# Ordering transfers one behind the other, casting four batches ahead, and widening a quarter-array layout to two more batches

## The chip, the cores and the metric

The kernel runs on one core of one Trainium2 chip. The metric is device time in microseconds (us). A run's median and range cover all of its executions. Engines are named as in the profile: PE is the TensorE (PEld its weight loads), DVE the VectorE, ACT the ScalarE, POOL the GpSimd, SP the SyncE, which here only issues transfers.

## The reference

Eight batches, eight heads, 576 positions, 64 features. Each head has two attentions, whose outputs are added: one on q, k and v averaged over groups of four positions, repeated back to 576, and one local, over neighbours closer than four positions. The result, 4608 tokens of 512 features, goes through a two-layer feed-forward block.

```python
def _attn_ref(q, k, v):                       # each (8, 8, 576, 64) fp32
    q_d = q.reshape(B, H, 144, 4, D).mean(axis=3)        # also k_d, v_d
    out_up = np.repeat(sm_attn(q_d, k_d, v_d), 4, axis=2)
    mask = np.abs(pos[:, None] - pos[None, :]) < 4
    ...                                       # softmax of the masked scores, times v
    return out_up + out_local

def _moe_ref(x, w_in, w_out):                 # x (4608, 512), w_in (512, 2048), w_out (2048, 512)
    h = x @ w_in
    g = 0.5 * h * (1.0 + erf(h * inv_sqrt2))
    return g @ w_out
```

## The kernel before

The tokens go through the two layers in nine chunks of 512 rows. In each chunk `m1` is the first layer with its gelu, `m2` the second. The attention of the next batch `b = c + 1` is woven into the second layer: it calls `fill(n)`, which puts n second-layer matmuls between its own short ones, so that the PE has something to do while exponentials and masks are made elsewhere. During `m1` the VectorE prepares the batch (`prep`, or `prep_q` for batches from BQ on): sums of four, and copies of values and keys.

A batch's data come in three steps. The **cast** copies keys and queries from fp32 to fp16 in device memory, on GpSimd's transfer queue. The **transposes** (`qk_turn`) bring them into the on-chip memory with features on partitions, from SP's queue. The **value loads** (`v_load`) are transfers on GpSimd's queue, among them `v_grp` and `v_lo` (values grouped by four) and `v_win` (windows of 64 positions). In the traces each engine goes through its instructions in the order of the program. On GpSimd a one-element copy onto `hold` waits for its operand, and so holds back everything behind it.

```python
def qk_cast(b, names=("kn", "qn")):
    for nm in names:
        t = dpool.tile([S, H, D], F16, tag=f"{nm}{0 if b == 2 else 1 - b % 2}", bufs=1, name=nm[0] + "16")
        nc.gpsimd.dma_start(out=t, in_=(k if nm == "kn" else q)[b].rearrange("h s d -> s h d"))
        v16[nm, b] = t
        ...

def qk_turn(b):
    for nm in ("kn", "qn"):
        nc.sync.dma_start_transpose(out=xT_of(b, nm), in_=v16[nm, b].rearrange("s h d -> s (h d)"))

# one attention on the full array
def attn(b, fill):
    fill(6)
    scores(b, 0)
    s_lo(b)
    fill(6)
    mask(0)
    for p in range(NP):                      # four groups of two heads
        if p + 1 < NP:
            scores(b, p + 1)
            mask(p + 1)
            ...
            fill(2)
        else:
            fill(4)
        av(b, p)                             # values and sums
        norm_out(b, p)
        ...

# ... the main loop
for c in range(NCH):
    b = c + 1
    f1 = filler(m1(c)) if c else f1_0
    ...
    if b == 1:
        qk_turn(2)
        v_load(2)
    elif b < B:
        (prep_q if b >= BQ else prep)(b)
    if 1 < b < B - 1:
        nc.gpsimd.tensor_copy(out=hold, in_=KL[0:1, 0:1] if b < BQ else qd[0:1, 0, 0:1])
        if b < BQ:
            qk_cast(b + 1)
        v_load(b + 1)
        if b == BQ - 1:
            qk_cast(7)
        qk_turn(b + 1)
    f1()
    f2 = filler(m2(c))
    if b < B:
        to_exp()
        (attn_q if b >= BQ else attn)(b, f2)
    f2()
```

For batches 6 and 7 (BQ = 6) the attention runs on quarters: matmuls of 64x64 placed on the four quarters of the 128x128 array, several at once (in the trace of the kernel before four of them start within 0.03 us, at 212.68 us, and take 0.20 us each). That is less time for the PE (an undisturbed stretch, as defined below, takes 32.00 us in place of 32.70) and far more instructions: 437 matmuls per chunk in place of 245.

## Time and profile before

| what | before |
|---|---|
| time, median of 3 runs (range) | 325.49 us (324.43 to 326.04) |
| span of the profiled execution, mean granted clock | 322.9 us, 0.995 |
| PE busy | 312.4 us, 97% |
| stretches of batches 2 to 7 | 33.40, 32.70, 32.70, 32.70, 37.40, 32.00 us |

A stretch goes from the start of one chunk's first layer to that of the next; stretch b carries the attention of batch b. The prediction below shows these lines and reads them. One more view matters for what came after: the timeline of GpSimd in the kernel before, around the preparations of batches 5 and 6 (columns: start, duration, engine, line, operation, output<-input, count, and in brackets the idle time before it with what ended it).

```profile
170.45 0.20 POOL L894 COPY hold<-KL 1x1 f16<-1x1 f16 x1 [11.45 <-DVE KL L347]
170.71 2.21 POOL L167 DMA_DIRECT2D k<-in_k_dram  x1
172.40 2.74 POOL L167 DMA_DIRECT2D q<-in_q_dram  x1
174.10 1.93 POOL L154 DMA_DIRECT2D v_grp<-in_v_dram  x1
...
203.49 0.18 POOL L894 COPY hold<-qd 1x1 f16<-1x1 f16 x1 [6.77 <-DVE qd L386]
203.97 0.91 POOL L154 DMA_DIRECT2D v_grp<-in_v_dram  x1 [0.30 <-issue]
```

Here a batch's grouped values stand behind two cast transfers at most (or none), and are issued a whole stretch before they are summed. The view of that tile has them landing 10.5 to 15.6 us after issue, over seven batches. So in the kernel before no load of grouped values was late: nothing on the PE or the VectorE waited for `v_grp`.

### The profile page before, as it was taken

To read this page: it belongs to the slowest core of one execution; us is meant where nothing else is said; L and a number is where in the kernel's file an instruction comes from. 1 tells how busy PE (TensorE), PEld (TensorE's weight loads), DVE (VectorE), ACT (ScalarE), POOL (GpSimd) and SP (SyncE) were. 2 spreads that over 40 slices of the span, in tenths; PEclk is the share of its full clock that TensorE was granted. 3 is DMA by queue.
4 is the path that set the end of the run, shared out by engine and by line. 5 is a ranking of instruction groups with operands and counts; after the bars stand their busy time and mean duration, and the time that the engine had idled before them with its cause. 6 is when DMAs were issued, how large, how long until landed. Compare 5 with 4: busy or idle time off the path is not lost.

```text
span 322.9 us, 6805 instructions
## 1 busy us (share of the span) xinstructions
PE 312.4 (97%) x2803; PEld 162.0 (50%) x2803; DVE 176.6 (55%) x395; ACT 220.2 (68%) x381; POOL 114.2 (35%) x145
## 2 busy tenths in 40 slices
PE   8899999999999999999999999995999999999995
PEld 3565655544654565446545554452444544444444
DVE  7575777539875757675795479935492640000001
ACT  6676977777886788678867886764576677415610
POOL 8968478332912564065308353630000000000000
PEclk9999999999999999999999999999899999999999
DMA  6999999999999599979999999999200120020011
GB/s 86 147 184 177 202 196 159 163 145 181 124 164 159 145 161 141 185 119 168 147 228 62 173 144 208 167 153 154 98 9 0 37 100 0 0 99 32 0 67 65
DMA packets 155454, 39.96 MB, mean 124 GB/s; under 512 B 137376, under 2 KB 150944, under 8 KB 155424
## 3 DMA queue, kind: packets, MB, share of 16 engines
q0 software_dynamic: 122064, 23.02, 90.0%
q1 hardware_dynamic: 33360, 16.52, 27.9%
q8 instruction: 22, 0.36, 0.5%
q14 instruction: 8, 0.07, 0.1%
HBM read 46.01 MB, written 16.52 MB: 194 GB/s over the span
## 4 chain that ended last, share of the span: by engine, by line
PE 77%; DMA 15%; POOL 3%; issue 2%; DVE 2%; POOLq 0%; DVEq 0%
PE m_ps L283 36%; PE m_ps L252 26%; DMA w_in_sb<-in_moe_w_in_dram 6%; PE m_first L244 4%; DMA q_nat<-q 4%; DMA v_grp<-in_v_dram 3%; DMA w_out_sb<-in_moe_w_out_dram 3%; PE nm L561 2%; PE sc L551 1%; PE sc L533 1%; POOL old L214 1%; PE m_ps L274 1%; PE sc L449 1%; DVE qd L308 1%; PE nm L558 1%
## 5 line engine op out<-in xcount | busy, mean ns | idle before, releaser
L283 PE MATMUL m_ps<-w_out_sb,gT 128*128 128x512 f16 x544 | 128.4, 383 | 0.4 <-DMA w_out_sb<-in_moe_w_out_dram 0.4
L252 PE MATMUL m_ps<-xT,w_in_sb 128*128 128x512 f16 x504 | 111.9, 379 | 0.0
L255 ACT ACTIVATE gT<-m_ps 128x512 f16<-128x512 f32 x126 | 75.2, 597 | 30.7 <-PE m_ps L252 30.5
L283 PEld LDWEIGHTS <-gT 128*128 128x128 f16 x544 | 50.3, 98 | 55.3 <-issue 2.9
L252 PEld LDWEIGHTS <-w_in_sb 128*128 128x128 f16 x504 | 48.6, 98 | 58.0 <-issue 1.4
L144 POOL DMA_DIRECT2D v_win<-in_v_dram x40 | 33.2, 972 | 30.7 <-DMA q<-in_q_dram 14.6
L278 DVE COPY out_sb<-m_ps 128x256 f32<-128x256 f32 x2 | 0.8, 424 | 54.4 <-PE m_ps L274 54.4
L287 ACT COPY out_sb<-m_ps 128x512 f32<-128x512 f32 x21 | 12.3, 584 | 26.0 <-PE m_ps L283 25.8
L576 DVE TENSOR_TENSOR xl<-nm,lr 128x576 f16<-128x576 f32 x20 | 15.2, 758 | 17.5 <-ACT lr L572 17.5
L591 DVE TENSOR_TENSOR xT<-xl,up 128x576 f16<-128x576 f16 (+8 forms) x41 | 22.1, 565 | 0.8
L707 POOL DMA_DIRECT2D v_win<-in_v_dram x20 | 14.6, 896 | 14.6 <-DMA v_grp<-in_v_dram 4.3
L545 DVE TENSOR_TENSOR e<-e,band 128x576 f16<-128x576 f16 x20 | 9.1, 453 | 14.6 <-ACT e L540 14.6
L167 POOL DMA_DIRECT2D q<-in_q_dram x6 | 15.9, 2652 | 0.4 <-DMA w_out_sb<-in_moe_w_out_dram 0.4
L244 PE MATMUL m_first<-xT,w_in_sb 128*128 128x512 f16 x64 | 15.1, 379 | 0.0
L894 POOL COPY hold<-KL 1x1 f16<-1x1 f16 x4 | 0.8, 204 | 40.0 <-DVE KL L347 40.0
L571 ACT ACTIVATE lr<-lr 128x576 f32<-128x576 f32 x20 | 13.7, 683 | 0.6
L247 ACT ACTIVATE gT<-m_first 128x1024 f16<-128x1024 f32 x8 | 8.2, 1024 | 8.6 <-PE m_first L244 8.6
L539 ACT ACTIVATE ed<-sc 128x288 f16<-128x288 f32 x20 | 8.1, 407 | 8.3 <-PE sc L533 8.3
L167 POOL DMA_DIRECT2D k<-in_k_dram x6 | 13.3, 2209 | 0.8 <-DMA v_win<-in_v_dram 0.5
L488 DVE TENSOR_TENSOR xl<-nm,lr 128x576 f16<-128x576 f32 x8 | 6.1, 758 | 13.6 <-ACT lr L484 13.6
L570 ACT ACTIVATE lr<-sc 128x576 f32<-128x576 f32 x20 | 13.1, 657 | 0.0
L540 ACT ACTIVATE e<-sc 128x576 f16<-128x576 f32 x20 | 12.9, 644 | 0.0
(233 smaller groups left out, 475.5 us busy)
## 6 DMA issues: line engine op xcount, KB each, us to landing
out_dram<-out_sb SPq DMA_DIRECT2D x35, 256.0 KB, 5.9
v_grp<-in_v_dram POOLq DMA_DIRECT2D x7, 512.0 KB, 12.4
k<-in_k_dram POOLq DMA_DIRECT2D x6, 576.0 KB, 8.5
q<-in_q_dram POOLq DMA_DIRECT2D x6, 576.0 KB, 11.1
v_win<-in_v_dram POOLq DMA_DIRECT2D x40, 72.0 KB, 9.9
w_in_sb<-in_moe_w_in_dram POOLq DMA_DIRECT2D x4, 512.0 KB, 9.1
w_out_sb<-in_moe_w_out_dram POOLq DMA_DIRECT2D x4, 512.0 KB, 9.0
v_win<-in_v_dram POOLq DMA_DIRECT2D x20, 64.0 KB, 11.6
```

The lines of the kernel that those rows point to most:

```text
L144: nc.gpsimd.dma_start(out=vw[64 * hh:64 * hh + 64, 0:9, p, 64 * hh:64 * hh + 64], in_=bass.AP(x.tensor, x.offset, [[D, 64], [57 * D, 9], [ ...
L167: nc.gpsimd.dma_start(out=t, in_=(k if nm == "kn" else q)[b].rearrange("h s d -> s h d"))
L244: nc.tensor.matmul(out=half[j], lhsT=w_in_sb[:, fc, 128 * j:128 * j + 128], rhs=xT[:, fc, x0:x0 + 512], start=(fc == 0), stop=(fc == 3))
L252: nc.tensor.matmul(out=ps, lhsT=w_in_sb[:, fc, 128 * j:128 * j + 128], rhs=xT[:, fc, x0:x0 + 512], start=(fc == 0), stop=(fc == 3))
L255: nc.scalar.activation(out=g[:, j, :], in_=ps, func=ACTF.Gelu)
L283: nc.tensor.matmul(out=ps, lhsT=g[:, j, 128 * t:128 * t + 128], rhs=w_out_sb[:, j, :], start=(j == 0), stop=(j == NJ - 1))
L540: nc.scalar.activation(out=e.rearrange("p (g c) -> p g c", g=2), in_=sc2[:, :, 0:SH], func=ACTF.Exp, scale=0.125)
L570: nc.scalar.activation(out=lr2, in_=sc2[:, :, 0:SH], func=ACTF.Ln)
L571: nc.scalar.activation(out=lr2, in_=lr2, func=ACTF.Exp, scale=-1.0)
L576: nc.vector.tensor_tensor(out=xl.rearrange("p (g c) -> p g c", g=2), in0=nm2[:, :, 0:SH], in1=lr2, op=ALU.mult)
L591: nc.vector.tensor_tensor(out=xT[:, p, y:y + z - a].rearrange("p (g r) -> p g r", r=4), in0=xl[:, a:z].rearrange("p (g r) -> p g r", r=4), ...
L707: nc.gpsimd.dma_start(out=quarter(b)["vw"][HS[g], i, :, :], in_=v[b, :, w:w + 64, :].rearrange("h s d -> s h d"))
```

## The change

The intent is to take traffic out of the late stretches, where something delayed the PE. The transposes go ahead of the value loads, and each kind of transfer behind the one before it; the casts of 4 to 7 move ahead, into the stretches of batches 2 and 3; batches 4 and 5 also run on quarters. Lesser parts: copies on the VectorE become maxima of an operand with itself, the constants of quarters are made a batch earlier, and the first second layer takes its matmuls in another order. The core of the diff (left out: a tile `bandq` of its own for the mask of quarters, `k_lo` moved up in `prep`, one more filler size):

```diff
-    BQ = 6
+    BQ = 4
@@ qk_cast
-            t = dpool.tile([S, H, D], F16, tag=f"{nm}{0 if b == 2 else 1 - b % 2}", bufs=1, name=nm[0] + "16")
+            t = dpool.tile([S, H, D], F16, tag=f"{nm}{b}", bufs=1, name=nm[0] + "16")
@@
+    def held(x):
+        nc.gpsimd.tensor_copy(out=hold, in_=x)
@@ qk_turn
-        for nm in ("kn", "qn"):
+        for nm in ("kn", "qn") if b == 2 else ("qn", "kn"):
@@ m2 of chunk 0
-            for t in range(2):
-                for j in range(NJ // 2):
+            for t, j0, j1 in ((0, 0, 8), (1, 0, 8), (0, 8, 12), (1, 8, 11)):
+                for j in range(j0, j1):
@@
+    def same(out, x):
+        nc.vector.tensor_tensor(out=out, in0=x, in1=x, op=ALU.max)
+
+    def quarter_consts():
+        ...                                  # moved here from prep_q
@@ attn, on the full array
-        fill(6)
+        fill(8 if b == 2 else 6)
@@ main loop
+        if 1 < b < B:
+            (prep_q if b >= BQ else prep)(b)
+        if b == BQ - 1:
+            quarter_consts()
         if b == 1:
             qk_turn(2)
+            held(xT_of(2, "qn")[0:1, 0, 0:1])
             v_load(2)
-        elif b < B:
-            (prep_q if b >= BQ else prep)(b)
-        if 1 < b < B - 1:
-            nc.gpsimd.tensor_copy(out=hold, in_=KL[0:1, 0:1] if b < BQ else qd[0:1, 0, 0:1])
+        elif b < B - 1:
+            if b == 2:
+                held(KL[0:1, 0:1])
+                qk_cast(3)
+            qk_turn(b + 1)
             if b < BQ:
-                qk_cast(b + 1)
+                held(xT_of(b + 1, "kn")[0:1, 0, 0:1])
             v_load(b + 1)
-            if b == BQ - 1:
-                qk_cast(7)
-            qk_turn(b + 1)
+            for n in {2: (4,), 3: (5, 6, 7)}.get(b, ()):
+                qk_cast(n)
```

## The prediction

> **What bounds the kernel now.** I read the page first, then busy time by stretch, then the order of the TensorE in time. The page says that the TensorE is the bound:
>
> ```profile
> PE 312.4 (97%) x2803; PEld 162.0 (50%) x2803; DVE 176.6 (55%) x395; ACT 220.2 (68%) x381; POOL 114.2 (35%) x145
> PE   8899999999999999999999999995999999999995
> PEclk9999999999999999999999999999899999999999
> DMA  6999999999999599979999999999200120020011
> ```
>
> No other engine passes 68%, so only three things can shorten the span: less TensorE work, a TensorE gap closed, or a slow clock avoided. There is one notch, in slice 28 (index 27, about 218 to 226 us), where the clock digit also dips. The DMA row is full until about 234 us and almost empty after it: transfers are crowded early, and the last third has room.
>
> I then cut the span where the first layer of each 512-row chunk starts (its first pair of banks, m_first). Each stretch is one chunk's two layers with the next batch's attention woven into the second layer. Columns: stretch, length, busy us (instructions) of PE, PEld, DVE, ACT, POOL, then clock, DMA share, GB/s.
>
> ```profile
> 63.10:96.50 33.40, 33.04 (x245) 17.22 (x244) 22.70 (x45) 25.82 (x47) 14.87 (x17) 1.00 1.71 154
> 96.50:129.20 32.70, 32.70 (x245) 17.21 (x244) 21.97 (x41) 25.61 (x47) 15.42 (x18) 1.00 1.56 152
> 161.90:194.60 32.70, 32.70 (x245) 17.23 (x244) 22.09 (x44) 25.61 (x47) 15.25 (x17) 1.00 1.52 150
> 194.60:232.00 37.40, 33.85 (x437) 16.16 (x436) 23.49 (x59) 23.29 (x38) 10.62 (x14) 0.95 1.57 161
> 232.00:264.00 32.00, 32.00 (x437) 15.67 (x436) 20.19 (x45) 23.17 (x39) 0.00 (x0) 1.00 0.10 35
> ```
>
> These carry batches 2, 3, 5, 6 and 7 (batch 4's is 32.70 too). Batches 6 and 7 already use quarters. A full-array stretch costs 32.70, an undisturbed quarter stretch 32.00. Batch 6's took 37.40, so it lost 5.4 us; batch 2's lost 0.7. The order in time shows where batch 6 lost it:
>
> ```profile
> 220.14 0.24 PE L421 MATMUL sc<-qd,kdt 64*64 64x72 f16 x6
> ...
> 223.93 0.22 PE L421 MATMUL sc<-qd,kdt 64*64 64x72 f16 x2 [3.54 <-issue]
> ```
>
> Six of eight score matmuls of one group ran, then nothing for 3.54 us, with no data, engine or buffer named: "issue". A data wait would not split a group whose operands are the same tiles. In program order the stopped instruction is number 4003 of 5608 in the TensorE's queue. The page's instruction queue moved 22 packets:
>
> ```profile
> q8 instruction: 22, 0.36, 0.5%
> ```
>
> 0.36 MB over 22 is 16 KB, that is 256 instructions of 64 bytes. I located all 22 in time and counted the TensorE instructions run by then: 21 come 49 to 173 instructions after numbers 163 + 256k, and one, k = 14, comes 331 after, at about 221 us. The next number of that series is 4003. So the TensorE ran into a block of instructions not yet there: the fetch, due at about 216.4 when the block before it was entered, was over at 223.9, some 7.5 us. The TensorE had crossed a block in under 4 us because quarters need many short instructions. Afterwards it ran half-clocked for a while: twelve second-layer matmuls took 4.38 us in the chain of waits, against 2.70 elsewhere. 3.54 + 1.68 = 5.2 of the 5.4.
>
> Why was the fetch late? Transfers were crowded. In batch 6's stretch the transposes and value windows for batch 7 ran together, after a hold that released only when prep 6 was done at 203.5. Output stores of 256 KB measure it: median time to landing in batch 6's stretch, then in batch 7's:
>
> ```profile
> out_dram<-out_sb SPq DMA_DIRECT2D x6, 256.0 KB, 7.0
> out_dram<-out_sb SPq DMA_DIRECT2D x4, 256.0 KB, 2.2
> ```
>
> [...] an idle of 3.54 us, then 0.79 mean clock from 224 to 232 us. [...]
>
> **The change part by part.**
> 1. *Batches 4 and 5 on quarters.* Two stretches go from 32.70 to 32.00: **-1.4 us**. The TensorE queue grows from 5608 to 6376 instructions, so 3 more block fetches.
> 2. *Casts ahead.* The cast of 4 moves into batch 2's stretch, those of 5, 6, 7 into batch 3's. From batch 4 on nothing holds the transposes and value loads, which start as soon as their buffers are free, at the stretch's start. For batch 6's stretch this leaves one pair of transposes (before: 12.5 to 14 us from issue to landing each) and about 7 us of value loads, begun at its start rather than 9 to 11 us into it. They should be over before attention 6, 14 us in. Attention 6 contains the same block alignment as before (a crossing at the 29th of 96 value and sum instructions, the next at the 13th of 16 score instructions, 3.9 us later), so only a fast fetch saves it. In batch 7's empty stretch four fetches cost nothing. **-5.4 us**.
> 3. *Transposes before value loads (batches 2 to 4).* Before, q of batch 2 landed at 75.8 because it shared engines with value loads; its sum ended at 78.5, and the first score waited 0.28; more went at the mask behind it. Batch 2's keys' sums now also go ahead, and attention starts two fillers later: **-0.5** of the 0.7.
> 4. *Reordered start of the first second layer.* The 0.43 us wait for the last quarter of w_out lay in the chain. Now 23 matmuls, not 20, precede its first use, at 0.216 each 0.65 us more: **-0.4**.
> 5. *Copies turned into maxima.* A 64x512 copy took 0.29; the two-operand form takes 0.68 for that many columns; four of them add 1.6 us of VectorE per quarter batch, the small ones 0.2. Prep 7 ended at 243.4, and value products come after 250. Off the path: **0**. The constants (about 2.4 us) move to batch 3's stretch, ahead of its first mask.
>
> Sum: -7.7 us, giving 317.8.
>
> **The rivals.**
> *The serial chain becomes the bound.* In batches 2 and 3 one transfer now waits for another: transpose pair, value loads (11 or 12 issues at about 0.75, so 9 us), cast (k and q: about 11 us alone). Batch 3's last transpose is now the keys', and the VectorE needs 8 us from there to the queries' sum (1.9 copies, 2.6, 0.6, 0.4, 2.6). Attention 3 wants it at about 110.3, so keys by 102. The cast of 3 starts near 79 to 81 and lands near 91. If an uncrowded pair of transposes takes 8 to 9 us, keys come at 100 and nothing is lost; if it still takes the 12 us of issue alone that it took before (6 + 6.4 to 8), they come at 105, and attention 3 stalls 3 us, the constants before the mask add perhaps 2, and batches 4 and 5 inherit some. That would leave 321 to 323. For it: every pair on record took at least 12 us of issue. Against: all of those were crowded; first packets moved 4.4 us after issue, as stores took 7 instead of 2.
> *The late fetch returns elsewhere.* Casts 5 to 7 (about 22 us of transfers) spill into batch 4's stretch while its attention runs in short instructions. Its crossings are about 6 us apart, against a crowded fetch of 4 to 7.5: 0 to 1.5 us. In attention 5 one pair is 4.1 us apart, when transfers should be done; if not, up to 3.5 plus the clock.
> *The 3.54 us was a data wait.* Then casts cannot cure it and about 323 remains. The arithmetic of 256 speaks against it.
>
> **Range and chances.** I charge 0.8 us for the first two rivals on average: 317.8 + 0.8 = 318.6. Everything clean gives 317; a stall of 3 to 4 us in batches 3 to 5 gives 322. Two per cent is 319.0, hardly above my number, so the verdict hangs on whether these stalls stay below 1.2 us: 0.56 faster, 0.41 same, 0.03 slower.
>
> **What would show it.** Right: no TensorE gap over 1 us after 50 us; stretches of 4, 5, 6 and 7 at 32.0 each, of 2 and 3 below 33; 25 instruction packets; clock 1.00 throughout. Wrong: a first-score or mask wait in batch 3's stretch behind a transpose (serial chain); an "issue" gap in attention 4 or 5 at numbers 163 + 256k (late fetch); batch 6's gap still there (cause misread).

## More of the kernel before

From the first layer, `m1`, the loop that two experiments change:

```python
    for j in range(2, NJ):
        ps = mm()
        for fc in range(4):
            nc.tensor.matmul(out=ps, lhsT=w_in_sb[:, fc, 128 * j:128 * j + 128],
                             rhs=xT[:, fc, x0:x0 + 512], start=(fc == 0), stop=(fc == 3))
            ...                              # gelu after fc == 3
```

## The result and the profile after

| | before | after |
|---|---|---|
| time, median of 4 runs (range; one more run of the kernel before than in the table above) | 325.76 us (324.43 to 328.01) | 338.74 us (337.82 to 341.73) |
| ratio to before, 95% interval | | 1.0407 (1.0319 to 1.0495): slower |
| span of the profiled execution, clock | 322.9 us, 0.995 | 337.5 us, 0.972 |

A ratio is the mean time of one kernel's fast runs over that of the other's in the same rounds, so it is not quite the ratio of the medians in the table. Executions over 1.5% slower than the fastest of the same kernel are left out of the means. The outputs are correct. The change costs 4%; the prediction had it gaining 2%.

The page of the kernel after, with the lines that answer to those which the prediction quotes (busy time by engine, then the span in 40 slices):

```profile
PE 311.6 (92%) x3187; PEld 159.5 (47%) x3187; DVE 175.5 (52%) x400; ACT 215.4 (64%) x365; POOL 113.7 (34%) x144
...
PE   7799999999999999999993069999999999999995
...
PEclk9999999999999999999999559999999999999998
DMA  6999999999999999999999999990100110011011
```

The PE has 0.8 us less to do than before and takes 14.6 us longer: there is one hole, 180.9 to 197.4 us into the span, and a halved clock in it and right after it (0.50 granted from 185.6 to 202.7 us). (The instruction queue moved 25 packets, as predicted.) Batches 2 and 3 took 33.04 and 33.34 us; the busy time by stretch for batches 4 to 6 (start:end, length, busy us and instructions of PE, PEld, DVE, ACT and POOL, then clock, DMA share and GB/s):

```profile
129.83:161.91 32.08, 32.08 (x438) 15.72 (x436) 20.39 (x44) 23.04 (x39) 24.37 (x22) 1.00 1.79 137
161.91:214.02 52.11, 34.99 (x437) 16.85 (x437) 20.97 (x47) 23.32 (x39) 17.92 (x27) 0.84 1.54 158
214.02:246.01 31.99, 31.99 (x437) 15.68 (x437) 20.77 (x44) 23.14 (x39) 4.16 (x7) 1.00 0.66 90
```

Nearly everything that went wrong is in batch 5's stretch. Against before: start of batch 2's stretch (62.93 by the first matmul of its first layer, now 63.45; the prediction cut at 63.10) +0.5, batches 2 to 7 -0.36, +0.64, -0.62, **+19.41**, **-5.41**, -0.02, the rest +0.4; the sum is the 14.6 us of the two spans. Batch 5's 52.11 consists of 32.0 for an undisturbed quarter stretch, 17.1 us in which the PE stood still (52.11 less 34.99 busy) and 3.0 us more busy time at a low clock (34.99 against 31.99, at a granted 0.84 against 1.00).

What did it stand still for? The order of the PE in time, and the VectorE's timeline:

```profile
177.60 0.45 PE L415 MATMUL sl<-qd,ex 128*128 128x144 f16 x4 [0.59 <-DVE ex L375]
...
197.39 0.46 PE L456 MATMUL sc<-e,ON 64*64 64x288 f16 x4 [16.52 <-DVE e L445]
```

```profile
171.84 2.55 DVE L392 TENSOR_REDUCE kdt<-k_nat 128x576 f16<-128x2304 f16 x1 [9.13 <-DMA k_nat<-k]
...
176.77 0.86 DVE L375 TENSOR_TENSOR ex<-kdt 64x32 f16<-64x32 f16 x8
191.19 0.69 DVE L371 TENSOR_TENSOR v_two<-v_grp 128x512 f32<-128x512 f16 x1 [13.56 <-DMA v_grp<-in_v_dram]
...
196.88 0.46 DVE L445 TENSOR_TENSOR e<-e,bandq 128x576 f16<-128x576 f16 x1
```

The PE waits for the masked exponentials `e`. The multiplication that makes them takes 0.46 us and needs no values at all, but it stands on the VectorE behind the sums of batch 5's values, and those wait 13.56 us for `v_grp` to land; the sums and copies behind it fill 191.19 to 196.88. So the VectorE passed a late operand on to work that does not read it. (The keys of batch 5 were late too: the VectorE waited 9.13 us for them, until 171.84. That alone cost the PE the 0.59 us for `ex`.) The chain of waits names the transfer:

```profile
158.58 32.59 DMA v_grp<-in_v_dram
```

From issue to landing 32.59 us, where the median of this tile is 7.0:

```profile
DMA to landing us min/median/max: 6.0/7.0/32.6
```

GpSimd's timeline tells why it was issued so late, and what was ahead of it. The buffers for batch 5's values were free at 129.8 us, when batch 3's attention ended.

```profile
140.14 2.26 POOL L168 DMA_DIRECT2D k<-in_k_dram  x1
...
152.54 2.19 POOL L168 DMA_DIRECT2D k<-in_k_dram  x1 [1.44 <-issue]
156.90 2.20 POOL L168 DMA_DIRECT2D q<-in_q_dram  x1 [2.17 <-issue]
158.58 1.40 POOL L155 DMA_DIRECT2D v_grp<-in_v_dram  x1
...
176.89 0.68 POOL L714 DMA_DIRECT2D v_win<-in_v_dram  x1 [10.69 <-DMA k<-in_k_dram]
188.05 0.68 POOL L714 DMA_DIRECT2D v_win<-in_v_dram  x1 [10.48 <-DMA q<-in_q_dram]
```

Six cast transfers are issued between 140 and 159 us; the grouped values of batch 5 come seventh. Issuing is not landing: at 176.89 and 188.05 GpSimd itself still waits for casts to end. Meanwhile SP issues the transposes of batches 5 and 6, whose packets move beside the casts' (the page counts both queues as shares of the same 16 engines): those of 5 are being issued from 152.3 to 165.5, those of 6 from 167.7 to 182.8. In the packet records GpSimd's queue moves about 1055 packets per us from 152 to 158 us, while SP's moves 82, and about 474 from 158 to 165.5, beside 314 of SP's.

So the traffic that was taken out of batch 6's stretch, which did become as short as predicted, was piled up ahead of batch 5's loads.

### The profile page after: what moved, and what is told of

It reads as the page before. It is cut to its first block, busy times and chain, and to the rows that moved or that the text cites.

```text
span 337.5 us, 7581 instructions
## 1 busy us (share of the span) xinstructions
PE 311.6 (92%) x3187; PEld 159.5 (47%) x3187; DVE 175.5 (52%) x400; ACT 215.4 (64%) x365; POOL 113.7 (34%) x144
## 3 DMA queue, kind: packets, MB, share of 16 engines
q1 hardware_dynamic: 33360, 16.52, 22.7%
HBM read 46.01 MB, written 16.52 MB: 185 GB/s over the span
## 4 chain that ended last, share of the span: by engine, by line
PE 62%; DMA 23%; DVE 8%; POOL 4%; issue 1%; ACT 1%; DVEq 0%; POOLq 0%
PE m_ps L287 29%; PE m_ps L256 22%; DMA v_grp<-in_v_dram 10%; DMA w_in_sb<-in_moe_w_in_dram 6%; DMA w_out_sb<-in_moe_w_out_dram 4%; PE m_first L248 3%; DMA v_win<-in_v_dram 2%; PE sc L456 2%; DMA k_nat<-k 1%; POOL old L218 1%; PE nm L456 1%; PE m_ps L278 1%; PE sc L434 1%; PE nm L568 1%; DVE kdt L308 1%
## 5 line engine op out<-in xcount | busy, mean ns | idle before, releaser
L287 PE MATMUL m_ps<-w_out_sb,gT 128*128 128x512 f16 x537 | 126.1, 384 | 0.0
L714 POOL DMA_DIRECT2D v_win<-in_v_dram x40 | 27.7, 735 | 35.4 <-DMA k<-in_k_dram 10.7
L490 ACT ACTIVATE lr<-sc 128x720 f32<-128x720 f32 x16 | 12.3, 770 | 36.9 <-PE sc L456 35.4
L456 PE MATMUL sc<-e,ON 64*64 64x288 f16 x64 | 5.2, 313 | 16.5 <-DVE e L445 16.5
L145 POOL DMA_DIRECT2D v_win<-in_v_dram x24 | 18.2, 840 | 5.8 <-DMA w_out_sb<-in_moe_w_out_dram 2.3
L168 POOL DMA_DIRECT2D q<-in_q_dram x6 | 15.2, 2533 | 4.2 <-issue 4.2
L168 POOL DMA_DIRECT2D k<-in_k_dram x6 | 14.5, 2410 | 1.7 <-issue 1.7
L445 DVE TENSOR_TENSOR e<-e,bandq 128x576 f16<-128x576 f16 x16 | 7.2, 451 | 15.0 <-ACT e L444 15.0
L392 DVE TENSOR_REDUCE kdt<-k_nat 128x576 f16<-128x2304 f16 x4 | 10.2, 2546 | 9.1 <-DMA k_nat<-k 9.1
L491 ACT ACTIVATE lr<-lr 128x720 f32<-128x720 f32 x16 | 12.8, 803 | 0.5
L371 DVE TENSOR_TENSOR v_two<-v_grp 128x512 f32<-128x512 f16 x8 | 5.5, 688 | 14.5 <-DMA v_grp<-in_v_dram 14.4
```

Source lines behind the costliest of these rows:

```text
L145: nc.gpsimd.dma_start(out=vw[64 * hh:64 * hh + 64, 0:9, p, 64 * hh:64 * hh + 64], in_=bass.AP(x.tensor, x.offset, [[D, 64], [57 * D, 9], [ ...
L287: nc.tensor.matmul(out=ps, lhsT=g[:, j, 128 * t:128 * t + 128], rhs=w_out_sb[:, j, :], start=(j == 0), stop=(j == NJ - 1))
L456: nc.tensor.matmul(out=out(g, hh), lhsT=lhsT(g, hh), rhs=rhs(g, hh), start=start, stop=stop)
L490: nc.scalar.activation(out=lr2, in_=sc2[:, :, 0:SH + DH], func=ACTF.Ln)
L491: nc.scalar.activation(out=lr, in_=lr, func=ACTF.Exp, scale=-1.0)
L714: nc.gpsimd.dma_start(out=quarter(b)["vw"][HS[g], i, :, :], in_=v[b, :, w:w + 64, :].rearrange("h s d -> s h d"))
```

## The experiments

The theory after the result, T: the loss comes from the order in GpSimd's stream, casts 5 to 7 ahead of batch 5's values. Its rivals: the transposes of 6, no longer held, delay the values (R1); quarters in batches 4 and 5 use up something that full-array attention did not (R2). A separate question was whether the prediction's reading of before, a late block of instructions, holds. All thirteen kernels gave correct outputs.

**a_two_later**: casts of 6 and 7 one pass later, behind batch 5's values.

```diff
-            for n in {2: (4,), 3: (5, 6, 7)}.get(b, ()):
+            for n in {2: (4,), 3: (5,), 4: (6, 7)}.get(b, ()):
```

> The changed kernel with the casts of batches 6 and 7 moved from batch 3's stretch to behind batch 5's value loads in batch 4's. Theory (the 16.5 us gap is batch 5's value loads standing behind the casts of 6 and 7 in GpSimd's queue): the grouped values of 5 land before 165 us, the gap before the sums of attention 5 goes, batch 5's stretch falls from 52.2 to 32 to 33 us, and the whole to 317 to 320 us. Rival 1 (transposes crowd out everything, whatever the order of the queue): casts, transposes and loads are the same in number, so a gap of over 5 us stays somewhere in batches 4 to 6 and the whole is over 325. Rival 2 (quarters need instructions faster than they are fetched): a gap at an instruction block, in batch 4 to 6.

Measured: 328.1 us (326.78 to 330.94, 14 runs), ratio to before 1.0073 (1.0043 to 1.0103). The 16.52 us gap is gone; `v_grp` takes at most 18.6 us. The ratio falls from 1.0407 to 1.0073, so some four fifths of the loss are back from moving two casts, as **T** has it. (As the transposes of 6 wait for the cast of 6, they moved too; m_turn6_late below takes the two apart.) The run missed its own 317 to 320 all the same: batch 5's stretch is 40.78 us long, for another reason. (The profiled execution is the slowest of the 14, 330.94: its clock was halved from 14 to 24 us as well, sixteen matmuls of `aw` taking 1.17 us at 17.7 us and 0.69 at 8.9, and batch 2's stretch began at 67.10.)

```profile
185.13 0.32 PE L456 MATMUL sc<-e,ON 64*64 64x288 f16 x4 [2.02 <-DVE e L445]
...
193.74 0.31 PE L434 MATMUL sc<-q_nat,k_nat 64*64 64x57 f16 x5 [4.17 <-issue]
```

The mask's wait that is left comes from batch 5's keys, not from its values, which landed at 165.3: the VectorE waited 7.38 us for the keys, until 173.12. Then the PE stops 4.17 us inside one group of score matmuls, with no data named: "issue", as in batch 6 before. It was not in the kernel after itself. There the clock was still halved behind the long hole (0.50 until 202.7 us), so that the PE took 6.3 us from the border before (198.0) to this one (204.3), with GpSimd's queue still busy (659 packets per us), where it takes 4.1 us here.

**b_one_later**: only the cast of 7 one pass later.

```diff
-            for n in {2: (4,), 3: (5, 6, 7)}.get(b, ()):
+            for n in {2: (4,), 3: (5, 6), 4: (7,)}.get(b, ()):
```

> The same with only the cast of batch 7 moved behind batch 5's value loads; that of 6 stays ahead of them. If the lateness grows with the bytes queued ahead of the value loads, one cast (1.2 MB written, 7.5 us alone, up to 15 us when it alternates with transposes) less makes the grouped values land 10 to 17 us earlier than 191 us: the gap of 16.5 us falls to between 0 and 5 us, the whole to 318 to 326 us. If the queue does not matter, it stays near 338.

(The 7.5 us for a cast alone are an estimate from the kernel after: two transfers of 576 KB at the 0.16 MB per us that its packet records show where GpSimd's queue moves alone, as from 155 to 156 us.)

Measured: 330.48 us (328.33 to 331.24), ratio 1.0133 (1.0081 to 1.0185). Between the two, as T has it for one cast pair more ahead of the values; `v_grp` takes at most 19.7 us. Three stops in batch 5's stretch, of 2.71 us for `ex`, 1.43 for `e` and 2.60 of "issue", in place of one of 16.5. The first two come from the keys again (the VectorE waited 11.24 us for them, until 174.26, and the values had landed at 170.6). The stops are in the range expected, the whole is not (318 to 326).

**d_no_quarters**: the kernel after with `BQ = 6`, the hold's condition kept at `b < 4`.

```diff
-    BQ = 4
+    BQ = 6
...
-            if b < BQ:
+            if b < 4:
                 held(xT_of(b + 1, "kn")[0:1, 0, 0:1])
```

> The changed kernel with quarters for batches 6 and 7 only, as before, and all of its transfers in the new order. Theory: the loss is in the transfers, so it is all still here: batch 5's stretch 50 to 54 us with the same wait behind its grouped values, the whole 338 to 341 us (the 1.3 us of quarters given back). Rival (quarters cause the gap): 318 to 322 us.

Measured: 339.54 us (337.28 to 342.12), ratio 1.0424 (1.0354 to 1.0495). The same loss without any quarters in batches 4 and 5, in the same place: `v_grp` takes up to 32.9 us, and the full-array attention waits nearly as long (14.58 us, after 2.81 for the queries' sums).

```profile
198.19 0.64 PE L558 MATMUL sc<-e,ON 128*128 128x288 f16 x2 [14.58 <-DVE e L552]
```

**R2 falls.** The casts' place is the cause, whatever the layout of the attention.

**m_turn6_late**: made last, to separate T from R1. The kernel after, but the transposes of 6 are issued only behind the output stores of batch 5's stretch. The casts stay where they were.

```diff
             ...
-            qk_turn(b + 1)
+            if b != 5:
+                qk_turn(b + 1)
             ...
         f2()
+        if b == 5:
+            qk_turn(6)
```

> The kernel after, with the transposes of batch 6 issued only behind the output stores of batch 5's stretch; the casts of 5, 6 and 7 stay ahead of batch 5's values. It tells how much of the 32.6 us landing of v_grp of batch 5 is the casts ahead of it in the queue, and how much the transposes of 6 that share the engines (167.7 to 183 us in the kernel after). If the order in the queue alone is the cause, v_grp is still issued near 158.6 and lands after 185, and the PE's wait for the mask stays above 12 us. If the transposes of 6 alone are the cause, it lands before 172 and the wait is under 1 us. Shared, which I hold likeliest: the casts of 5 and 6 and the transposes of 5 gave a landing of 19.7 us in the run with one cast moved; a third cast pair alone takes about 11 us, so a landing near 178 to 182 and a PE wait of 4 to 8 us. Batch 6's stretch gets longer by some us, as its keys come late; that is no part of the question.

Measured: 337.72 us (335.85 to 338.5), ratio 1.0341 (1.0276 to 1.0406). `v_grp` was issued at 159.31 as before and landed after 23.7 us, not 32.6:

```profile
189.20 0.45 PE L456 MATMUL sc<-e,ON 64*64 64x288 f16 x4 [7.65 <-DVE e L445]
```

The shared case, as expected: of the 16.52 us, 8.9 go with the transposes of 6, and 7.65 remain with the casts ahead and the transposes of 5 alone. Those 7.65 are not the values' alone, since the VectorE waits first for the keys of 5 and then for the values:

```profile
172.51 2.55 DVE L392 TENSOR_REDUCE kdt<-k_nat 128x576 f16<-128x2304 f16 x1 [9.04 <-DMA k_nat<-k]
...
183.00 0.69 DVE L371 TENSOR_TENSOR v_two<-v_grp 128x512 f32<-128x512 f16 x1 [4.69 <-DMA v_grp<-in_v_dram]
```

In run a, where the keys came as late (173.12) and the values in time, 2.02 us were left. **R1 has a part of about half, and only as long as the casts are ahead**: in a and b the values of 5, issued at 146.7 and 150.9, had landed before the transposes of 6 began (181.3 and 170.6). The time hardly moved, since batch 5's stretch became 8.7 us shorter (43.39) and batch 6's 7.2 longer (39.17), its keys now being late.

**c_quarters_only**: the kernel before with `BQ = 4` and nothing else (the casts' conditions kept at 6 and 5).

```diff
-    BQ = 6
+    BQ = 4
...
-            if b < BQ:
+            if b < 6:
                 qk_cast(b + 1)
             v_load(b + 1)
-            if b == BQ - 1:
+            if b == 5:
                 qk_cast(7)
```

> The kernel before with quarters for batches 4 and 5 alone (transfers in the old order). Theory: two stretches 0.6 to 0.7 us shorter, but attention 4 and 5 now run many short instructions among crowded transfers, so the late fetch of an instruction block can come back: 324 us if it does not (325.5 less 1.4), up to 329 if one more gap of 2 to 3.5 us with a slow clock appears. Rival (quarters caused the loss of the whole change): 335 or more.

Measured: 330.03 us (329.44 to 331.13), ratio 1.0124 (1.0076 to 1.0172), a little above the 324 to 329 expected. Quarters alone cost 4 us: stretches 4, 5 and 6 take 33.31, 37.34 and 37.35 us. There are now two stops of the old kind:

```profile
189.22 0.24 PE L427 MATMUL sc<-q_nat,k_nat 64*64 64x57 f16 x5 [3.35 <-issue]
...
230.14 0.34 PE L427 MATMUL sc<-q_nat,k_nat 64*64 64x58 f16 x17 [2.93 <-issue]
```

In the PE's program they fall at instructions 3757 and 4781 (each matmul counted with its weight load). Both are 173 beyond a multiple of 256; 4003 in the kernel before is 163 beyond one. Every other such stop of over 0.4 us is 163 beyond (kernels with 5608 to 5768 instructions) or 173 beyond (those with more). Stops that keep to multiples of 256 while tiles and batches change are stops for instructions.

**f_before_shift**: the test of the prediction's reading of before. In chunk 0, 36 first-layer matmuls of the kernel before are cut into two halves of 256 columns each. That adds nothing to compute, but 72 instructions to the PE's stream (5608 to 5680), so the borders of 256 fall elsewhere in batch 6's attention.

```diff
+            cut = 256 if c == 0 and j < 11 else 0
+            for fc in range(4 if cut else 0):
+                nc.tensor.matmul(out=ps[:, 0:cut], lhsT=..., rhs=xT[:, fc, x0:x0 + cut], start=(fc == 0), stop=(fc == 3))
             for fc in range(4):
-                nc.tensor.matmul(out=ps, lhsT=..., rhs=xT[:, fc, x0:x0 + 512], ...)
+                nc.tensor.matmul(out=ps[:, cut:512], lhsT=..., rhs=xT[:, fc, x0 + cut:x0 + 512], ...)
```

> The kernel before with 36 matmuls of the first layer's first chunk cut in two halves of 256 columns: 72 more TensorE instructions some 180 us ahead of attention 6, nothing else changed. Theory (its 3.5 us gap is a late block of 256 instructions): block borders move 72 instructions back in attention 6, where consecutive borders are then 6.5 to 7 us apart instead of 4, so the gap shrinks to under 1 us with no slow clock after it; batch 6's stretch 32 to 33.5 us instead of 37.4, the whole 320 to 322.5 us (0.2 to 1 us for the extra instructions). Rival (a data or bank wait at that place in the program): the gap stays at the seventh of eight score matmuls of the fourth group, the whole 325.5 to 327.

Measured: **321.67 us** (321.12 to 321.99), ratio 0.9846 (0.9818 to 0.9874), the fastest kernel. The stretch of batch 6, and what is left of the stop:

```profile
194.97:227.99 33.02, 32.33 (x438) 15.85 (x436) 24.30 (x60) 23.43 (x40) 11.31 (x15) 1.00 1.69 182
```

```profile
221.09 0.21 PE L453 MATMUL nm<-e,v_win 64*64 64x58 f16 x2 [0.47 <-issue]
```

37.40 became 33.02 us at the same traffic (161 GB/s before, 182 here), and the clock stayed at 1.00. Two borders that lay 3.9 us apart now lie 6.7 us apart. The fetch, counted as the prediction does from the border before to the end of the stop, takes 7.4 us (213.7 to 221.1) and is still late by 0.47, but no longer by 3.54. Batch 2's stretch begins 0.8 us later; half of that is a longer wait for `w_out` (0.82 us against 0.43).

**l_shift_control**: the rival to that reading would be that additional instructions help in some other way. So 160 instructions are added to the kernel before, rather than 72, which puts two borders about 4 us apart again, at another group of scores.

```diff
-            cut = 256 if c == 0 and j < 11 else 0                          # as in f
+            cut = 256 if c == 0 and j < 11 or c == 1 and j < 13 else 0
```

> Control for the shifted kernel before: 80 first-layer matmuls of the first two chunks cut in halves instead of 36, so 160 more TensorE instructions. By the count a border then lies after 6 of the 20 local score matmuls of attention 6's third group (one group earlier than in the kernel before), with the border ahead of it again about 4 us away. Theory (spacing of block borders, not the mere presence of extra instructions, decides): a stop of 2 to 4 us marked issue at that place, none at the fourth group, batch 6's stretch 35.5 to 38 us, the whole 324.5 to 328 us. Rival (cut matmuls help by themselves, for example by pace or data timing): no stop, the whole 321 to 323 us.

Measured: 327.21 us (325.56 to 328.93, 20 runs), ratio 1.0034 (1.0015 to 1.0053). The stop stands where the arithmetic put it, after 6 of the 20 local scores of the third group:

```profile
217.06 0.25 PE L431 MATMUL sc<-q_nat,k_nat 64*64 64x58 f16 x6
221.74 0.42 PE L431 MATMUL sc<-q_nat,k_nat 64*64 64x58 f16 x14 [4.43 <-issue]
```

Batch 6's stretch took 38.67 us at a clock of 0.91 (stop and stretch are a little over the ranges expected, the whole within its own). Same kernel, same traffic; **the spacing of the borders decides**, not the number of instructions.

Spacing is half of it; the other half is traffic. The count and the packet records of all fifteen traces settle it, from 60 us on. Nine times two borders lay 4.1 us apart while 490 to 990 packets per us were moving: the PE stopped all nine times, for 1.84 to 4.43 us. Twenty-six times they lay 4.1 or 4.2 us apart with at most 37 packets per us, as in the attention of batch 7: it never stopped.

**e_even**: one cast per pass, always behind the next batch's values.

```diff
-            for n in {2: (4,), 3: (5, 6, 7)}.get(b, ()):
+            for n in {2: (4,), 3: (5,), 4: (6,), 5: (7,)}.get(b, ()):
```

> The changed kernel with one cast in each of batch 2 to 5's stretches (of batches 4, 5, 6, 7), always behind the next batch's value loads. Theory: nothing stands ahead of batch 5's values, so the 16.5 us gap goes as it did with the casts of 6 and 7 put back; and with the transfers spread, none of the 4 us stop at an instruction block that appeared there: stretches of batches 4 to 7 at 32 to 32.5 us, the whole 317 to 320 us. If the late instruction block is a matter of the TensorE's pace alone and not of crowding, the stop of 2.5 to 4 us plus a slow clock stays in attention 5 (15 of 20 local score matmuls of its third group done, as in both runs before) and the whole is 322 to 326.

Measured: 325.92 us (322.9 to 327.72, 20 runs), ratio 0.9984 (0.9957 to 1.001). All of the loss is back, and none of the gain came, so its 317 to 320 is missed: batch 5's stretch still takes 37.32 us, with a wait of 2.61 for the mask (the keys came at 170.06, after 7.96 us of waiting on the VectorE) and a stop for instructions of 0.46. That stop is small here because the clock was halved behind the mask's wait (twelve second-layer matmuls took 4.45 us, in place of 2.76), so that the borders lay 5.8 us apart in place of 4.1. (One execution of 20 was profiled, at 324.04.)

**g_even_consts**: e, with the quarters' constants made in batch 4's pass again, out of batch 3's VectorE work.

```diff
+        if b == BQ:
+            quarter_consts()
         if 1 < b < B:
             (prep_q if b >= BQ else prep)(b)
-        if b == BQ - 1:
-            quarter_consts()
```

> The same as the even casts, with the quarters' constants (15 small VectorE instructions) written at the start of batch 4's preparation rather than behind batch 3's, where they held up the first mask of attention 3 by 0.47 us in the changed kernel. Theory: batch 3's stretch goes from 33.3 to 32.7 to 32.8 us, batch 4's stays at 32.1 because its first mask has the slack; the whole 0.3 to 0.7 us below the even casts. If the late landing of batch 3's keys, not the constants, sets that wait, nothing changes.

Measured: 325.54 us (322.95 to 328.27), ratio 0.9972 (0.9937 to 1.0006). Nothing that shows was gained over e (the intervals overlap): batch 3's stretch is 32.71 in both profiles, so e had no wait behind the constants to remove. Batch 5 lost 1.43 to the mask and 3.31 to instructions here; the sums of its keys waited 6.78 us for the transposes.

**h_even_no_holds**: g without the two holds that keep value loads back until the transposes have landed. This asks which of the two should go first.

```diff
             qk_turn(2)
-            held(xT_of(2, "qn")[0:1, 0, 0:1])
             v_load(2)
...
             qk_turn(b + 1)
-            if b < BQ:
-                held(xT_of(b + 1, "kn")[0:1, 0, 0:1])
             v_load(b + 1)
```

> The same as the last, without the holds that let value loads of batches 2, 3 and 4 start only when the transposes have landed. Theory of the change (transfers one behind the other are faster): without them a transpose pair takes 13 us or more from issue to landing again instead of 8, and batch 2's stretch goes back from 33.0 to 33.4 us or batch 3's keys come late; the whole 0.5 to 3 us longer. Rival (the holds gain nothing, since loads and transposes share the engines either way): the same within 0.5 us, or shorter.

Measured: 323.87 us (321.44 to 328.0, 20 runs), ratio 0.9921 (0.9894 to 0.9948). Shorter than g and not longer, which is what its rival expected. In the profiles batches 2 and 3 do lose 1.2 and 0.85 us against g (34.25 and 33.56), so the holds are worth more there than the 0.5 us that the prediction counted. Batch 5 gains 3.0 (35.76 against 38.76): with holds everything behind them in GpSimd's stream comes later (SP issues the transposes of 5 at 152.69 us in g, at 138.08 here); without them the keys of 5 cost no wait, and the stop for instructions is 1.84 us.

**j_even_two_holds**: g with the holds only ahead of the value loads of batches 2 and 3, to have both.

```diff
-            if b < BQ:
+            if b < 3:
                 held(xT_of(b + 1, "kn")[0:1, 0, 0:1])
```

> The even casts with the constants at batch 4, and the holds kept only for batches 2 and 3 (there they gained 0.6 to 1.2 us a stretch), not for batch 4's value loads, where the chain they make let batch 5's keys land late (a mask wait of 1.4 and 2.6 us in attention 5 with the holds, none without). Theory: stretches of 2, 3, 4: 33.0, 32.7, 32.1; batch 5's has no mask wait but still the late instruction block (15 of 20 local score matmuls of its third group), 34 to 38 us; the whole 321 to 324 us. Rival (the mask wait in attention 5 came from the casts, not from the holds): a mask wait over 1 us stays there.

Measured: 325.89 us (323.08 to 327.63), ratio 0.9987 (0.996 to 1.0014). A miss as a whole; batch 5's stretch (36.38 us, no mask wait, the late block) went as expected. The wait moved into batch 4, whose keys the VectorE waited 6.18 us for:

```profile
149.94 0.32 PE L456 MATMUL sc<-e,ON 64*64 64x288 f16 x4 [2.97 <-DVE e L445]
...
188.89 0.24 PE L434 MATMUL sc<-q_nat,k_nat 64*64 64x57 f16 x5 [2.41 <-issue]
```

**i_aligned**: j, with 76 first-layer matmuls in chunks 3 and 4 cut as in f, to spread the borders in batch 5.

```diff
+            cut = 256 if c == 4 or c == 3 and j < 7 else 0
             ...                              # the two halves as in f
```

> The same, with 76 first-layer matmuls cut in two halves (20 in batch 4's stretch, 56 in batch 5's): 40 and 152 more TensorE instructions ahead of attentions 4 and 5, so that by the instruction count consecutive 256-instruction borders in attention 5 are 5.4 to 6 us apart instead of 4. Theory: the stop at an instruction block goes or falls under 1.5 us and the slow clock with it; batch 5's stretch 32.2 to 34 us, the whole 318 to 320.5 us, 2 to 5 us under the run without the cuts. Rival (with four transfers crowded, no spacing is enough): a stop of over 2 us at another place in attention 4 or 5, no gain over 1 us.

Measured: 325.13 us over all 20 runs (321.14 to 328.83), of which eight count as slow; the ratio of the fast ones is 0.9926 (0.9899 to 0.9953). A miss of its 318 to 320.5 (leaving eight out flatters the ratio; the medians of all runs differ by 0.3%). Batch 5's stretch, 33.91 us, was within its 32.2 to 34. In the profiled run the clock was 1.00 and the two stops for instructions were 0.81 and 1.54 us, together as much as j's one of 2.41, though without a slow clock behind them (the next twelve second-layer matmuls took 2.76 us, behind j's stop 4.45); the wait for the mask in batch 4 stayed, at 2.23. As the runs spread over 7 us, I take no finer reading from it.

**k_even_no_quarters**: j with `BQ = 6`, that is with full-array attention in batches 4 and 5 (the constants are made at the end of batch 5's preparation, as the kernel after makes them at the end of batch 3's).

```diff
-    BQ = 4
+    BQ = 6
```

> The even casts and two holds, with batches 4 and 5 on the full array as in the kernel before. Theory: full-array attentions cross a block of 256 instructions in 6 to 17 us, so no stop at a block in batches 4 and 5, and batch 6's attention starts after the transfers: stretches 33.0, 32.7, 32.7, 32.7, 32 to 33, 32.0, the whole 319 to 321 us; quarters on 4 and 5 then cost 2 to 4 us more than they give (1.3) as long as transfers are crowded. Rival (the transfers' order is the loss): over 323.

Measured: 322.72 us (321.89 to 323.88), ratio 0.9893 (0.9843 to 0.9943). That misses the 319 to 321 expected, by one stretch. No stop for instructions at all. Only batch 4 waits for its transposed data, its stretch being 35.65:

```profile
147.08 0.28 PE L536 MATMUL sc<-qd,kdz 128*128 128x144 f16 x2 [2.04 <-DVE qd L313]
```

Against j (325.89), quarters in batches 4 and 5 cost about 3 us while traffic is dense, where the prediction counted a gain of 1.4.

## Why the prediction was wrong

**What bounds the kernel, and the late block: right.** c, f and l show it in three ways: the stop repeats with other batches on quarters, shrinks when two borders are moved apart and comes back where the arithmetic says. "-5.4" for batch 6 was measured as -5.41, and for the reason given: the two borders are 3.9 us apart there (235.9 to 239.8), and hardly a packet is moving (1 per us). It is no gift of the long hole: a, b and e, which have none, take 31.97 or 31.98 us there. The block of 256 instructions fits the pages of both profiles: 0.36 MB in 22 packets for 5608 instructions before, 0.41 MB in 25 for 6376 after, which is 255 instructions a packet and 64 bytes each. Two details do not come out of the trace. The value loads are 12 issues, not 11 or 12. Counted by the matmuls begun, the 21 packets come from 43 instructions before the prediction's numbers to 141 after them, and the one at 221 us comes 255 after, with the PE already standing before 4003; the conclusion is the same. A slow clock was measured behind a shorter stop than the 3.54 us of before, too: behind one of 1.84 us in h, twelve second-layer matmuls took 4.30 us, against 2.76 ahead of it.

**Part 2, casts ahead: this is the step that failed.** The prediction says that from batch 4 on nothing holds "the transposes and value loads, which start as soon as their buffers are free, at the stretch's start". For batch 5's values this is false. Their buffers were free at 129.8 us; they were issued at 158.58, behind six cast transfers in the same stream, and landed at 191.17. It is false for batch 5's transposes too: they had to wait for the cast of 5, were issued at 152.29, 22.5 us into batch 4's stretch, and brought the keys at 171.84. No term of the sum stood for this; it measured +19.41 us in batch 5's stretch (20.1 against a clean quarter stretch). The order of GpSimd's issues after the change could be read before any run. The prediction did count "casts 5 to 7 (about 22 us of transfers)" and said they spill into batch 4's stretch, but used this for instruction fetches alone, not for the loads queued behind. Runs a, b, d and m show it: with two casts moved behind the values the 16.52 us wait is 2.02; with one moved it is 1.43, after 2.71 for `ex`; with no quarters, it is 14.58. What a and b have left comes from the keys. Run m adds that the transposes of 6, which the prediction was content to let go early, made about half of the wait, by moving beside what the values stood behind (`v_grp` landed 32.6 us after issue with them, 23.7 without).

**Part 1, quarters: right for batch 4, not beyond.** -0.62 against the -0.7 counted for each. In batch 5 the stall swamped it. The price of 3 more blocks was listed, and charged only as a part of the 0.8 us for two rivals; c and the pair j and k show that it is 3 to 4 us when transfers are dense.

**Part 3, transposes first: nearly right.** -0.36 against -0.5. Batch 3 lost 0.64, of which 0.47 us were a wait for the mask. It takes both of the things that the prediction names: keys that the VectorE waited 1.60 us for (until 98.89), and behind them the constants, 3.5 us of it. In e the constants stand at the same place, the keys are there at 97.3, and nothing is lost. So the place was right and the size (3 and 2) too large.

**Part 4, first second layer: not seen.** Counted -0.4; batch 2's stretch starts 0.5 us later. A wait for `w_out` of 0.48 us is still there: it moved rather than vanished.

**Part 5, maxima for copies: right that they cost nothing, on a wrong size.** They took 0.41 to 0.42 us per 64x512, not 0.68, so 0.5 us in place of 1.6 over four.

**The rivals.** The serial chain hardly bound: the uncrowded pair of transposes took 8.2 us from the first issue (90.72) to the landing of the keys (98.89), the favourable one of the two cases named, and its share is in the 0.47 us above. The late fetch in batches 4 and 5 is not in the kernel after, where the halved clock behind the stall (0.50) had spread the borders (6.3 us apart); in a, b, c, e, g, h, i, j and m it appears, at 0.46 to 4.17 us, in some of them with a slow clock behind it. The range was wrong because a data wait behind casts in GpSimd's own stream was not among the rivals. The sum assumed that transfers taken out of a late stretch cost nothing where they go.

**Open.** Why one fetch takes 6.2 us (e) and another 8.5 (l), counted from the border before, beside transfers of both queues, and why e to j spread 5 to 8 us between runs, was not settled. Transposes are not needed for a late fetch: in h, i (the stop of 1.54) and m the packet records show GpSimd's queue alone, but for one output store, and the fetches took 5.9, 6.9 and 6.5 us; which transfers delay one most stays open. How much of the loss is owed to the hold ahead of batch 4's values was not run on the kernel after: GpSimd stands in it until 129.39 and issues the cast of 5 from 140.14 on (in j, without it, from 126.05). No version was found that has f's alignment and k's order at once, and f's 321.67 us stands as the best measured.

## What to carry to other kernels

Before you move a transfer ahead, write down the order of that engine's whole stream after the change and ask of each later load when it is issued and what lies before it in the queue; here a prefetch placed ahead of a load that was needed sooner delayed it (32.6 us to landing behind six casts, at most 18.6 in run a with two of them moved behind it), and the VectorE handed the delay on to work that does not need the data (its 13.56 us of waiting for values became 16.52 us on the PE). Put a prefetch behind the loads of the batch that comes first. Where a gap shows "issue" inside one group of equal instructions, count the instruction's number in the program: if it keeps to multiples of 256 while transfers are dense (490 to 990 packets per us here), a few instructions more or fewer upstream, to spread the borders, can be worth more than a change of the schedule (here 1.5%, with 72 instructions added).

## What the traces show of fetches, transfers and the VectorE

- Fetches of instructions. Beside dense transfers there were stops of 0.46 to 4.43 us, fetches of some 5.9 to 8.5 us (an estimate, worked out from where the borders lie and when the stop ended), and a stop each of the nine times that two borders lay about 4 us apart. Borders 6.7 us apart cost 0.47. With at most 37 packets per us under way borders about 4 us apart cost nothing, 26 times.
- Transfers of different issuers. The same 512 KB of grouped values took 6.0 us and 32.6 us from issue to landing in one run (the longer one with six casts ahead of it in its own queue; 23.7 without the transposes of 6 beside them, run m), and a transpose's issue 3.0 us alone and 5.6 to 8.2 beside casts.
- The VectorE beside GpSimd. One tensor-scalar operation of 128x256 on the VectorE took 0.29 us in the kernel before and 1.83 us in the kernel after, where GpSimd was issuing a cast; there it ended 0.1 us after that issue did (113.44 and 113.31 us).
- Quarters. They brought more instructions per us (437 matmuls in a stretch that had 245), and with them borders of blocks closer together (one each 9.4 us on average in place of 17.1, worked out from these counts and the stretches of 32.00 and 32.70 us; 3.9 us in batch 6's attention); here quarters in two more batches cost 3 to 4 us (runs c, and j against k) where the busy time alone promised a gain of 1.4.
